# K^T transposes of an attention backward kernel issued one tick later on SyncE

## The chip, the cores and the metric

The kernel runs on one core of a Trainium2 chip. Its time is the device time of one execution in microseconds (us); the time before is the median of three runs, 1651.42 us (1650.91 to 1652.69). A profile and a trace of one further execution are at hand.

## The reference

Two independent attention blocks, A and B, are computed forward and differentiated. Each has x (8 x 96 x 640), key and value caches of 8 batches x 32 heads x 512 keys x 128, and the weights wq (640 x 4096) and wo (4096 x 640), all in bfloat16. The forward part of a block is

```
q      = (x @ wq) split into 32 heads of 128
scores = einsum("bhqd,bhkd->bhqk", q, k_cache) * 128 ** -0.5
p      = softmax(scores)
o      = einsum("bhqk,bhkd->bhqd", p, v_cache)
out    = (o, heads joined) @ wo
```

The kernel returns the two outputs side by side (8 x 96 x 1280) and, for a given grad_out of that shape, the gradients of x, k_cache, v_cache, wq and wo of both blocks (the vector-Jacobian product of this function).

## The kernel before

**Work items and ticks.** The unit of work is one (block, head, batch) triple: 2 x 32 x 8 = 512 items, each with 96 queries and 512 keys. A small class (`Emitter`) collects pieces of work under (tick, slot) and writes them out sorted by tick, then slot, then order of entry. One item starts per tick, so a head takes eight ticks, and a tick lasts about 1651 / 512 = 3.2 us on average. The table `OFF` says how many ticks before or after its item's own tick each stage of an item is issued, and `SLOTS` orders the stages in a tick. The items overlap as a software pipeline: while one item's scores are computed, others are in their later stages.

**Stages of an item.** K and V of two neighbouring batches, a pair, are loaded together (`c_ld`, 256 KB each; K five ticks ahead of the pair's tick, V three). Two operands are needed with the other axis on the partitions: K^T for the scores, V^T for dP. They are made by a DMA transpose from SBUF to SBUF, again for a pair at once (`c_xt`, L272 to L278, line L275 in the profile). For some items TensorE makes K^T instead, from the loaded K, with a copy by VectorE (`c_s1`): for the first pair of every head of even number, for all of head 0 of each block and for head 1 of block A (`k_on_pe`, L556). So 214 of the 256 pairs have a DMA transpose of K, and all 256 have one of V.

Three ticks after its own tick an item gets its scores (`c_s2a`, L298: S_ps<-KT,QT_h on TensorE, then the row maximum on VectorE), the exponential on ScalarE (L310), the reciprocal (L320, VectorE) and the scaled P (L329, GpSimd). Four ticks after: dV = P^T dO (L389), copied out by ScalarE (L392). Five: O^T from V and the transposed P (L359). Six: dP from V^T and dO (L417), then dS (L421). Seven: dK = dS^T Q (L432, copied out L435) and the transpose of dS. Eight: dQ^T from K (L340). Stores of dV and dK go out for a pair at a time, one tick after the second item's stage (`c_st`, L398).

**Work per head and per group.** Each head also has its slices of wq and wo loaded (L190, L199), transposed on TensorE and multiplied with x and grad_out (L243); later dwo (L469) and, for two heads at once, dwq (L490). The output and dx are summed over groups of about five heads (L514). These pieces sit in slot 90 and above, at the end of their ticks, so that ticks differ in length.

**SyncE's queue.** All DMAs are issued by SyncE, in the written order: most of them are pinned to it (`pinned`), and so are the transposes. Within a tick the loads of K and V come first (slot 0), then the transposes (slot 1), then the stores of dV and dK (1.5), the stores of dwo and dwq (1.6) and the loads of wq and wo (1.7). Heads start at odd ticks and pairs at every second tick, so V loads, K loads and dK stores fall in even ticks, and V^T transposes and dV stores in odd ticks. Before an issue SyncE waits until the data is there and the buffer free. Buffers are counted in pairs: seven for K, five for V, four each for K^T and V^T, four each for dK and dV.

Each transpose reads a tile of 128 x (2 x 4 x 128) and writes one of 128 x 8 x 128; a K^T buffer becomes free when the score matmuls of the pair four DMA transposes earlier are done, a V^T buffer when the dP matmuls of the pair four earlier are.

The table and the lines that place the transposes:

```
OFF = dict(ldk=-5, ldv=-3, kt=-3, vt=0, s2=3, s3=3, s4=4, s5=5, s6=6, s7=7, s8=8)
...
if not k_on_pe(h, b):
    em.add(ct + OFF["kt"], SLOTS["LOAD"] + 1, c_xt(h, b, "KT", 4))
em.add(ct + OFF["vt"], SLOTS["LOAD"] + 1, c_xt(h, b, "VT", 4))
```

Here `ct` is the tick of the pair's first item.

Of the kernel before, what the change touches and what calls it, by code (L numbers as in the profile page):

```python
# [41 lines left out]
SL_GRP = 95  # L42
SL_SETUP = 96

OFF = dict(ldk=-5, ldv=-3, kt=-3, vt=0, s2=3, s3=3, s4=4, s5=5, s6=6, s7=7, s8=8)
HK = dict(pA=-10, pA2=-9, pB=-3, pC0=[-2, 0], pC1=[-1, 0], pD1=1, pD0=2, qA0=18, qA1=17, qB=[19, 20], qD=[(18, 0, 2), (19, 2, 4), (21, 4, 5)])
EV = dict(pB0="act", pB1="dve", pC00="act", pC01="act", pC10="act", pC11="dve", pD0="dve", pD1="dve", qA0="act", qA1="dve", qB0="act", qB1="dve", qD="dve", gU="act")
GSPREAD0 = 9
# [5 lines left out]
def build_block(tc, em, tick0, blk, x, kc, vc, wq, wo, g_all, out_all, dx, dk, dv, dwq, dwo, ident, ones, pools, HG=6, first=True, groups=None):  # L54
# [207 lines left out]
    def c_ld(h, b, n, bufs):  # L262
        def f():
            src = kc if n == "K" else vc
            X = kvp.tile([128, NB, KC, 128], BF16, name=n + "_sb", bufs=bufs)
            pinned(nc.sync.dma_start(X[:], src[b:b + NB, h].rearrange("b (p c) d -> p b c d", c=KC)))
            for i in range(NB):
                st = CS.setdefault((blk, h, b + i), {})
                st[n + "_sb"], st[n + "_all"] = X[:, i], X
        return f  # L270

    def c_xt(h, b, name, bufs):  # L272
        def f():
            XT = kvp.tile([128, NB * KC, 128], BF16, name=name, bufs=bufs)
            pinned(nc.sync.dma_start_transpose(XT[:], CS[(blk, h, b)][name[0] + "_all"][:].rearrange("p a c d -> p (a c d)")))  # L275
            for i in range(NB):
                CS[(blk, h, b + i)][name] = XT[:, i * KC:(i + 1) * KC].rearrange("p c k -> p (c k)")
        return f  # L278

    def c_s1(h, b):  # L280
        def f():
            st = CS[(blk, h, b)]
            kT_ps = bank([128, Sk], BF16, "kT_ps")
            for c in range(KC):
                nc.tensor.transpose(kT_ps[:, c * 128:(c + 1) * 128], st["K_sb"][:, c, :], ident[:])
            KT = wk.tile([128, Sk], BF16, name="KT_pe", bufs=2)
            nc.vector.tensor_copy(KT[:], kT_ps[:])
            st["KT"] = KT[:]
        return f

    def c_s2a(h, b):
        def f():
            with tc.high_priority(PRIO_OFF):
                st = CS[(blk, h, b)]
                hs = HS[(blk, h)]
                tok = slice(b * Sq, (b + 1) * Sq)
                S_ps = bank([Sq, Sk], F32, "S_ps")
                nc.tensor.matmul(S_ps[:], hs["QT_h"][:, tok], st["KT"], start=True, stop=True)  # L298
                negm = wk.tile([Sq, 1], F32, name="negm", bufs=3)
                nc.vector.tensor_reduce(negm[:], S_ps[:], axis=AX.X, op=ALU.max, negate=True)  # L300
                st["S_ps"], st["negm"] = S_ps, negm
        return f

    def c_s2b(h, b):
        def f():
            with tc.high_priority(PRIO_OFF):
                st = CS[(blk, h, b)]
                E_sb = wk.tile([Sq, Sk], BF16, name="E_sb", bufs=2)
                rowsum = wk.tile([Sq, 1], F32, name="rowsum", bufs=3)
                nc.scalar.activation(E_sb[:], st["S_ps"][:], ACT.Exp, bias=st["negm"][:], scale=1.0, accum_out=rowsum[:])  # L310
                st["E_sb"], st["rowsum"] = E_sb, rowsum
                del st["S_ps"]
        return f

    def c_s3a(h, b):
        def f():
            with tc.high_priority(PRIO_OFF):
                st = CS[(blk, h, b)]
                rinv = wk.tile([Sq, 1], F32, name="rinv", bufs=3)
                nc.vector.reciprocal(rinv[:], st["rowsum"][:])  # L320
                st["rinv"] = rinv
        return f
# [233 lines left out]
    def k_on_pe(h, b):  # L556
        return (b // NB == 0 and h % 2 == 0) or h == 0 or (first and h == 1)

    SX = pools["SX"]
    for g in range(NG):  # L560
        h0 = GH0[g]
        for hh in range(groups[g]):
# [17 lines left out]
            for b in range(B):  # L580
                ct = c0t + b
                if b % NB == 0:
                    em.add(tick0 - 12 if first and h == 0 and b == 0 else ct + OFF["ldk"], SLOTS["LOAD"], c_ld(h, b, "K", 7))
                    em.add(ct + OFF["ldv"], SLOTS["LOAD"], c_ld(h, b, "V", 5))
# [3 lines that stand above are left out]
                if k_on_pe(h, b):  # L588
                    em.add(ct + 2, SLOTS["S1"], c_s1(h, b))
                em.add(ct + OFF["s2"], SLOTS["S2A"], c_s2a(h, b))  # L590
                em.add(ct + OFF["s2"], SLOTS["S2B"], c_s2b(h, b))
                em.add(ct + OFF["s3"], SLOTS["S3A"], c_s3a(h, b))
# [162 lines left out]
```

## Time and profile before

| what | value |
|---|---|
| time, median of 3 runs | 1651.42 us (1650.91 to 1652.69) |
| the profiled execution's own time | 1653.38 us |
| its span, first to last instruction | 1651.2 us |
| granted TensorE clock, mean | 0.998 |
| TensorE matmuls (PE) busy | 1633.2 us, 99% |
| ScalarE (ACT) / VectorE (DVE) / GpSimd (POOL) busy | 1391.9 / 1283.2 / 527.9 us |
| DMA: moved, mean rate | 447.11 MB, 271 GB/s |
| K^T transposes, issue to landing (median) | 4.7 us |
| V^T transposes, issue to landing (median) | 4.5 us |

The profile is of one execution. A line such as L275 is a line of the kernel; `out<-in` names the tile written and the tiles read. PE is TensorE's matmuls, PEld its weight loads; SPq is SyncE's queue, which only issues DMAs: the duration of such a row is the time that the issue took, and the data lands later. In lists in order of time the first column is the start in us from the span's start, the second the duration in us, and a bracket at the end tells how long the engine had been idle and what ended that. In lists of waits the numbers are the total in us, how often, and the longest. A busy TensorE isn't one at its peak, since the ends of matmuls are modelled.

### The profile page before, as it was taken

Reading aid. Unit: us, or ns where it says so; the run is one execution under the profiler, and the core shown is the slowest. Engines: PE = TensorE matmul, PEld = TensorE weight load, DVE = VectorE, ACT = ScalarE, POOL = GpSimd, SP = SyncE. Lnnn points to the kernel's source line nnn. Section 1 sums busy time; section 2 is a strip of 40 time slices with the busy share of each in tenths; the row PEclk is TensorE's granted clock in tenths of the full one; section 3 lists DMA queues with packets and bytes.
Section 4 is the critical chain, followed back from the end, with each engine's and each line's share of the span. In section 5 each row is a group of like instructions: output and inputs, shape, how many; then the busy total and the mean of one; then the engine's idle time right before and its main releaser. Section 6 shows DMA issues by size and latency. Waiting matters only on the chain.

```text
span 1651.2 us, 55679 instructions
## 1 busy us (share of the span) xinstructions
PE 1633.2 (99%) x21288; PEld 1303.0 (79%) x21288; DVE 1283.2 (78%) x2916; ACT 1391.9 (84%) x3518; POOL 527.9 (32%) x1034
## 2 busy tenths in 40 slices
PE   8999999999999999999999999999999999999999
PEld 6887787788788787887878877877877877877886
DVE  6886677788787787878878767778878778787777
ACT  6998898798798797988869998978977977987985
POOL 2332233232233232333323323323322322332332
PEclk9999999999999999999999999999999999999999
DMA  9999999999999999999999999999999999999995
GB/s 258 270 268 283 277 284 271 279 274 283 246 277 269 276 273 264 267 278 259 299 289 283 283 281 272 278 281 271 276 275 260 278 296 246 282 282 245 265 275 157
DMA packets 843947, 447.11 MB, mean 271 GB/s; under 512 B 516512, under 2 KB 843680, under 8 KB 843680
## 3 DMA queue, kind: packets, MB, share of 16 engines
q1 hardware_dynamic: 843680, 443.56, 110.8%
q8 instruction: 167, 2.74, 0.7%
q14 instruction: 100, 0.82, 0.1%
HBM read 161.09 MB, written 159.12 MB: 194 GB/s over the span
## 4 chain that ended last, share of the span: by engine, by line
PE 74%; ACT 15%; issue 5%; DVE 3%; DMA 2%; POOL 0%; SPq 0%; ACTq 0%; DVEq 0%; POOLq 0%
PE o_ps L514 12%; PE q_ps L243 10%; PE dwq_ps L490 6%; PE dK_ps L432 5%; PE dV_ps L389 5%; PE dP_ps L417 5%; PE S_ps L298 5%; PE dwo_ps L469 4%; PE dst_ps L346 4%; PE x_ps L365 4%; PE x_ps L359 4%; PE x_ps L340 4%; ACT dK_sb L435 3%; ACT E_sb L310 3%; ACT PT_sb L378 3%
## 5 line engine op out<-in xcount | busy, mean ns | idle before, releaser
L329 POOL TENSOR_SCALAR P_sb<-E_sb,rinv 96x512 bf16<-96x512 bf16 x512 | 353.6, 691 | 1096.3 <-DVE rinv L320 1062.1
L310 ACT ACTIVATE E_sb<-S_ps,negm 96x512 bf16<-96x512 f32 x512 | 354.4, 692 | 132.7 <-DVE negm L300 128.9
L421 DVE SCALAR_TENSOR_TENSOR dS_sb<-dP_ps,dl_ps,P_sb 96x512 bf16<-96x512 f32 x512 | 380.9, 744 | 46.7 <-PE dl_ps L419 42.4
L300 DVE TENSOR_REDUCE negm<-S_ps 96x1 f32<-96x512 f32 x512 | 347.5, 679 | 46.0 <-PE S_ps L298 43.9
L435 ACT ACTIVATE dK_sb<-dK_ps 128x512 bf16<-128x512 f32 x512 | 305.7, 597 | 89.1 <-PE dK_ps L432 88.1
L392 ACT ACTIVATE dV_sb<-dV_ps 128x512 bf16<-128x512 f32 x512 | 314.6, 614 | 0.0
L378 ACT ACTIVATE PT_sb<-x_ps 128x384 bf16<-128x384 bf16 x512 | 256.4, 501 | 0.0
L514 PEld LDWEIGHTS <-OD 128*128 128x128 bf16 x1536 | 135.7, 98 | 103.3 <-issue 1.3
L389 PE MATMUL dV_ps<-dOnat_h,P_sb 96*128 96x128 bf16 x2048 | 197.9, 219 | 1.0 <-DVE dOnat_h L160 0.6
L432 PE MATMUL dK_ps<-Qnat_h,dS_sb 96*128 96x128 bf16 x2048 | 197.8, 219 | 0.0
L417 PE MATMUL dP_ps<-VT,dOT_h 128*96 128x512 bf16 x512 | 195.3, 381 | 0.3
L407 POOL TENSOR_TENSOR prod<-OD,dOT_h 128x96 bf16<-128x96 bf16 x512 | 186.6, 364 | 9.2 <-ACT OD L375 8.2
L348 DVE COPY dST_sb<-dst_ps 128x384 bf16<-128x384 bf16 x512 | 177.1, 346 | 11.6 <-PE dst_ps L346 11.6
L320 DVE RECIPROCAL rinv<-rowsum 96x1 f32<-96x1 f32 x512 | 80.0, 156 | 133.3 <-ACT E_sb L310 128.6
L375 ACT ACTIVATE OD<-x_ps 128x192 bf16<-128x192 f32 (+1 forms) x515 | 171.4, 333 | 3.4 <-PE x_ps L340 3.4
L346 PE MATMUL dst_ps<-ident,dS_sb 96*128 96x96 bf16 x2048 | 171.8, 206 | 2.4 <-DVE dS_sb L421 0.2
L359 PE MATMUL x_ps<-PT_sb,V_sb 128*128 128x96 bf16 x2048 | 172.2, 206 | 0.5 <-ACT PT_sb L378 0.5
L365 PE MATMUL x_ps<-ident,P_sb 96*128 96x96 bf16 x2048 | 171.7, 205 | 0.5 <-POOL P_sb L329 0.3
L340 PE MATMUL x_ps<-dST_sb,K_sb 128*128 128x96 bf16 x2048 | 170.7, 206 | 0.0
L298 PE MATMUL S_ps<-KT,QT_h 128*96 128x512 bf16 x428 | 162.1, 379 | 1.1 <-DMA KT<-K_sb 0.7
L340 PEld LDWEIGHTS <-K_sb 128*128 128x128 bf16 x2048 | 133.3, 98 | 34.6
L514 PE MATMUL o_ps<-wo_h,OD 128*128 128x128 bf16 (+1 forms) x768 | 141.0, 299 | 0.0
(75 smaller groups left out, 3137.9 us busy)
## 6 DMA issues: line engine op xcount, KB each, us to landing
out_dram<-dV_sb SPq DMA_DIRECT2D x256, 256.0 KB, 3.5
out_dram<-dK_sb SPq DMA_DIRECT2D x256, 256.0 KB, 3.8
K_sb<-in_A_k_cache_dram SPq DMA_DIRECT2D x128, 256.0 KB, 4.1
V_sb<-in_A_v_cache_dram SPq DMA_DIRECT2D x128, 256.0 KB, 3.8
K_sb<-in_B_k_cache_dram SPq DMA_DIRECT2D x128, 256.0 KB, 4.1
V_sb<-in_B_v_cache_dram SPq DMA_DIRECT2D x128, 256.0 KB, 4.0
out_dram<-dwo_sb SPq DMA_DIRECT2D x64, 160.0 KB, 3.8
out_dram<-dwq_sb SPq DMA_DIRECT2D x32, 320.0 KB, 4.0
```

What stands on the lines that cost most here:

```text
L300: nc.vector.tensor_reduce(negm[:], S_ps[:], axis=AX.X, op=ALU.max, negate=True)
L310: nc.scalar.activation(E_sb[:], st["S_ps"][:], ACT.Exp, bias=st["negm"][:], scale=1.0, accum_out=rowsum[:])
L329: pinned(nc.gpsimd.tensor_scalar(P_sb[:], st["E_sb"][:], st["rinv"][:], 0.0, op0=ALU.mult, op1=ALU.add))
L340: nc.tensor.matmul(dQT_ps, st["K_sb"][:, c, :], st["dST_sb"][:, c * Sq:(c + 1) * Sq], start=(c == 0), stop=(c == KC - 1))
L378: nc.scalar.activation(PT_sb[:], PT_ps, ACT.Identity, scale=1.0)
L389: nc.tensor.matmul(dV_ps[:, c * 128:(c + 1) * 128], P_sb[:, c * 128:(c + 1) * 128], hs["dOnat_h"][:, b * 128:(b + 1) * 128], start=True, s ...
L392: nc.scalar.activation(SB[(blk, h, b // 2, "v")][:, b % 2], dV_ps[:], ACT.Identity, scale=1.0)
L417: nc.tensor.matmul(dP_ps[:], hs["dOT_h"][:, tok], st["VT"], start=True, stop=True)
L421: nc.vector.scalar_tensor_tensor(dS_sb[:], dP_ps[:], dl_ps[:, 0:1], st["P_sb"][:], op0=ALU.subtract, op1=ALU.mult)
L432: nc.tensor.matmul(dK_ps[:, c * 128:(c + 1) * 128], dS_sb[:, c * 128:(c + 1) * 128], hs["Qnat_h"][:, b * 128:(b + 1) * 128], start=True, s ...
L435: nc.scalar.activation(SB[(blk, h, b // 2, "k")][:, b % 2], dK_ps[:], ACT.Identity, scale=1.0)
L514: nc.tensor.matmul(o_ps[:], src[:, t * 128:(t + 1) * 128], rhs, start=(hh == 0), stop=(hh == groups[g] - 1))
```

## The change

K^T transposes are issued two ticks before their pair's tick instead of three. That is an odd tick, the one in which the V^T transpose of the pair before is issued, and in the same slot; the V^T transpose was entered first and comes first.

```diff
-OFF = dict(ldk=-5, ldv=-3, kt=-3, vt=0, s2=3, s3=3, s4=4, s5=5, s6=6, s7=7, s8=8)
+OFF = dict(ldk=-5, ldv=-3, kt=-2, vt=0, s2=3, s3=3, s4=4, s5=5, s6=6, s7=7, s8=8)
```

Nothing else differs. On SyncE the DMAs of two ticks, one pair of each kind, are then issued in this order (per-head loads and stores left out):

| before | after |
|---|---|
| V load | V load |
| K load | K load |
| **K^T transpose** | dK store |
| dK store | V^T transpose |
| V^T transpose | **K^T transpose** |
| dV store | dV store |

## The prediction

> **What bounds the kernel now.** I read the first part of the page (busy time by engine), then who waited for whom on TensorE, then the rows of the K^T tile, then the SyncE queue and TensorE in order of time at the tightest place.
>
> First part of the page: TensorE (PE) has work in 99% of the span, so 1651.2 - 1633.2 = 18.0 us is all that it idles, start and end included.
>
> ```profile
> PE 1633.2 (99%) x21288; PEld 1303.0 (79%) x21288; DVE 1283.2 (78%) x2916; ACT 1391.9 (84%) x3518; POOL 527.9 (32%) x1034
> ```
>
> Of the waits (us in all, times, longest), only these two are of TensorE for a K^T transpose: 2.0 us in three places. A change of the transposes can therefore win 2.0 us of waiting at most, and lose more.
>
> ```profile
> PEld L298 <- DMA KT<-K_sb: 1.3, 2, 1.0
> ...
> PE S_ps L298 <- DMA KT<-K_sb: 0.7, 1, 0.7
> ```
>
> The transposes by line, and the K^T tile: min, median and max of an issue in ns; the last line is us from issue to landing of K^T.
>
> ```profile
> L275 SPq DMA_TRANSPOSE VT<-V_sb x256: 1231/1384/3427, 12.2 to 1611.0; - x128
> L275 SPq DMA_TRANSPOSE KT<-K_sb x214: 1231/1236/2621, 47.9 to 1605.8; - x107
> ```
>
> ```profile
> DMA to landing us min/median/max: 3.2/4.7/6.9
> ```
>
> SyncE is nearly full too: its 1732 DMA issues take 1403 us of the 1651, and the 16 DMA engines are busy over 90% in all but the last slice. So SyncE runs late in stretches where TensorE's ticks are short. SyncE in order of time (start, duration) at the worst of them:
>
> ```profile
> 938.85 0.42 SPq L266 DMA_DIRECT2D K_sb<-in_B_k_cache_dram  x1
> 939.32 1.34 SPq L275 DMA_TRANSPOSE KT<-K_sb  x1
> 940.76 0.56 SPq L398 DMA_DIRECT2D out_dram<-dK_sb  x1
> 941.37 0.65 SPq L199 DMA_DIRECT2D wo_h<-in_B_wo_dram  x1
> 942.12 3.04 SPq L275 DMA_TRANSPOSE VT<-V_sb  x1
> 945.25 0.53 SPq L398 DMA_DIRECT2D out_dram<-dV_sb  x1
> ```
>
> and TensorE at its end:
>
> ```profile
> 944.80 0.30 PE L469 MATMUL dwo_ps<-g_nat,Onat 128*128 128x320 bf16 x1
> 945.85 0.42 PE L298 MATMUL S_ps<-KT,QT_h 128*96 128x512 bf16 x1 [0.75 <-DMA KT<-K_sb]
> ```
>
> The K^T issued at 939.32 lands at 945.80 (6.48 us, a piece of the chain that ended last), and its score matmul starts at 945.85. Six ticks were planned between them; here 6.5 us, some two ticks, are left, and TensorE waits already.
>
> I paired every K^T landing with the first score matmul that reads it (both are in program order in the trace) and call the time between them the margin: median 8.6 us, under 4 us for 23 of 214, smallest 0.04. The small ones come in stretches: score matmuls at 106 to 143 us (smallest margin 0.64, at 122.6), 508 (2.71), 906 to 960 (0.12 at 926.5, 0.04 at 938.3 and 945.8), 1072 to 1085 (2.86), 1578 (2.83).
>
> **The change, part by part.** It removes and adds nothing; TensorE, ScalarE, VectorE and GpSimd keep their orders. Moved are 214 DMA transposes on SyncE's queue, each one tick later. Built, the order of a pair goes from V load, K load, K^T, dK store, V^T, dV store to V load, K load, dK store, V^T, K^T, dV store.
>
> 1. What K^T is moved past: the dK store (median issue 0.57 us, gap 0.09) and V^T (1.38, gap 0.09), 2.1 us, and once in a head each a wo load or a dwo store (0.5 to 0.7). Row by row (from the dK store's start to V^T's end, with its waits, and 0.09) the issue moves by 2.0 to 3.9 us, median 2.6. At 939.32: 945.15 + 0.09 - 940.76 = 4.5.
>
> 2. What is moved forward: dK stores and V^T, by the K^T issue of 1.2 us. V^T's smallest margin to the dP matmul is 2.9 us and grows; dK buffers are rewritten 1.2 us or more after their store landed. Both are already covered, so this wins nothing: V^T's cover is its six ticks to the dP matmul. The dV store, the next V and K loads keep their place: the same issues stand ahead of them.
>
> 3. Waits. V^T waits for the dP matmul that frees its buffer; K^T now stands behind that wait. In the trace V^T's issue met a real wait of this kind five times (3.5 us in all): 45 of 256 K loads are held by TensorE instead (57 us), and V^T follows 2.4 us behind. After the change V^T follows only 1.1 us behind and will be held more often, but only where SyncE has caught up, and there the K^T margin is above 6 us. It is no cost while margins stand so; if not, it is up to 1.3 us on the K^T behind it.
>
> 4. What it costs. The loss of a stretch is the largest (delay - margin) in it, not the sum: once TensorE is late by that much, the later transposes of the stretch have that much more. Two rows price the delay, neither of them a K^T behind a V^T, which the trace does not show.
> By the issue, each K^T keeping its own time from issue to landing: 2.97 - 0.64 = 2.33 at 122.6; 3.32 - 2.71 = 0.61 at 508.2; 4.48 - 0.04 = 4.44 at 945.8; 3.88 - 2.83 = 1.05 at 1578.4; others negative or covered. Sum 8.4 us.
> By the landing: K^T's issue now ends when V^T's did, with the same work issued ahead, so it lands when V^T did: 1.75 (at 129.3), 1.99 (at 945.8: V^T landed at 947.84) and 0.69 (at 1071.6). Sum 4.4 us.
> The place in the queue speaks for the second, K^T's longer time from the end of issue to landing (median 3.16 us against 2.74) for the first. I take the middle, 6.4 us. Ends: V^T's issue at its shortest, 1.23 us, because no K^T is just ahead of it, with K^T's own landing: 4.9; less than 4.4 if the landings come closer together, down to nothing. Upward: K^T landing as its slowest tenth does, 4.5 us after the issue (+1.35): 16.9; and if SyncE is held back by the late TensorE, so that each of the 13 places pays for itself by the first pricing: 20.9.
>
> The Trainium skill, "Advanced Engine Details and Errata", section on the X-Bar transpose (TRN2), says that transpose DMAs are as fast as regular ones. The trace's packets differ: 1,024 of 256 B at 18 ns for a transpose, 256 of 1,024 B at 46 ns for a copy of the same 256 KB, on 16 engines 1.15 us against 0.74. By that rule V^T would put 0.41 us less in front of K^T in each of the four stretches of the first pricing, and that sum would be 8.4 - 1.6 = 6.8 us.
>
> Against the profiled execution (1653.38 us, span 1651.2 and 2.2 around it) the sum is 1659.8. That execution lies 2.0 us above the median of the three runs, 1651.42, so on the median: 1651.4 + 6.4 = 1657.8. Under 0.2% (3.3 us), a change can't be told from none.
>
> **Rivals.**
> - Hidden anyway, not slower: the transposes in the crowded stretches are held by the DMA engines, not by the queue. At 939.32 the K^T's first packets run only from 942.3, and nearly all engines then stand still from 942.8 to 944.7 in its middle. If that standstill falls on V^T when V^T goes first, K^T lands right behind it and only the 0.12 and 0.04 margins pay. For: it is a single piece of 2 us in the worst place. Against: V^T in front then passes the standstill on to K^T, which waits in the same queue. It decides if K^T lands less than about 1.5 us later at 926.5 to 945.8; time: 0 to 3 us more, 1653.
> - Larger: two transposes in a row, each 1,024 small packets, land later than one behind copies. For: V^T issued within 0.8 us of a K^T has 2.5 us or more of issue in one case of ten, against 1.4 where 4 us or more lie between. Against: its median there is 1.38. With 2 us on every K^T landing the stretches cost 22 us, with 4 us 41 us: 1673 to 1693.
> - Faster: V^T's issue is above its shortest by 91 us in all, K^T's by 40. If the new order sheds much of it, SyncE is less late and all margins grow. For: 4 copies now stand between a K^T and the next V^T. Against: K^T takes V^T's place right behind a transpose, and TensorE has 2.0 us of such waits to give back: 1649.4 at best, within 0.2%. More than that would need gains on ScalarE or VectorE that no row shows.
>
> **How the numbers follow.** Forecast, 3.3 to 17 us slower: 0.58. Larger, over 17 us: 0.14. Hidden, within 0.2%: 0.22. Faster by over 0.2%: 0.06. So slower 0.72, same 0.22, faster 0.06. The range leaves out the faster case with the lower half of the standstill case, and the upper part of the larger one: 1651.5 to 1674.
>
> **What would show it.** Right: TensorE's waits at L298 for K^T grow from 2.0 us to 5 to 10, in the stretches 106 to 143, 906 to 960 and perhaps 508, 1072 and 1578, not spread evenly; K^T lands 2 to 3 us later against its score matmul (median margin near 6); K^T's issue takes over V^T's excess. Wrong: no L298 waits (hidden), L298 waits in every head (larger), or other lines of TensorE waiting for V, K or wo loads.

## The result, and the profile after

The changed kernel takes 1720.35 us, the median of 4 runs (1714.02 to 1731.27), against 1652.06 us, the median of four runs of the kernel before: a ratio of 1.0413, 95% interval 1.0384 to 1.0441. It is 68 us slower where 6.4 were forecast, and outside the range. The profiled execution took 1716.21 us, its span is 1714.0 us, 62.8 more than before.

First part of the page of the changed kernel, busy time by engine:

```profile
PE 1639.6 (96%) x21107; PEld 1309.6 (76%) x21288; DVE 1288.9 (75%) x2916; ACT 1396.6 (81%) x3518; POOL 528.5 (31%) x1034
```

TensorE now idles for 74.4 us of the span and not 18.0. (181 matmul records are missing from this trace. A kernel shown below, two_between, has the same gaps in its records and takes as long as before, and its PE reads 1622.4 us, some 11 too low. So of the 74.4 us some 11 aren't idle.) Its work is some 17 us longer than that kernel's; the granted clock, 0.992 against 1.000 there, makes 13 of these. And the lower clock follows from the waits: between the first and the last 10 us it drops to half seven times, six times for 3.4 us and once for 6.8, and each drop directly follows a stretch of 3.4 us in which TensorE idled for 2.05 us or more in a wait for K^T. (From 130.0 to 133.4 us it works for 1.35 us; from 133.4 to 136.8 the granted clock is 0.50.) Of the stretches of 3.4 us with no drop behind them none has more than 1.88 us of idle time. The kernel before has no drop between 11 and 1649 us.

The waits of the changed kernel say what TensorE idles for (us in all, times, longest):

```profile
PEld L298 <- DMA KT<-K_sb: 51.1, 29, 4.5
...
PE S_ps L298 <- DMA KT<-K_sb: 42.2, 25, 4.3
```

So the line was forecast rightly, K^T ahead of the score matmul at L298: on the weight load, which waits first, 1.3 us became 51.1. (The matmul's 42.2 us are the later part of the same waits.) The chain that ended last, its shares by engine before and after, has more DMA now and less ScalarE:

```profile
PE 74%; ACT 15%; issue 5%; DVE 3%; DMA 2%; POOL 0%; SPq 0%; ACTq 0%; DVEq 0%; POOLq 0%
```

```profile
PE 74%; DMA 11%; ACT 8%; DVE 3%; issue 3%; SPq 0%; POOL 0%; ACTq 0%; DVEq 0%; POOLq 0%
```

The transposes by line, and the last line of the K^T tile's view, from issue to landing:

```profile
L275 SPq DMA_TRANSPOSE KT<-K_sb x214: 1299/1977/4129, 48.5 to 1676.8; - x107
```

```profile
L275 SPq DMA_TRANSPOSE VT<-V_sb x256: 1237/1494/3182, 11.7 to 1679.9; - x128
```

```profile
DMA to landing us min/median/max: 3.2/4.7/6.2
```

Here are two surprises. A K^T takes no longer from issue to landing, 4.7 us as before. But its issue, now right behind a V^T, takes 1.98 us in the median and not 1.24, while V^T's median did not get shorter (1.49 us after, 1.38 before). A pair on SyncE in order of time, at an ordinary place of the changed kernel:

```profile
712.95 0.42 SPq L266 DMA_DIRECT2D V_sb<-in_A_v_cache_dram  x1
713.46 0.45 SPq L266 DMA_DIRECT2D K_sb<-in_A_k_cache_dram  x1
714.00 0.95 SPq L398 DMA_DIRECT2D out_dram<-dK_sb  x1
715.04 1.30 SPq L275 DMA_TRANSPOSE VT<-V_sb  x1
716.40 1.89 SPq L275 DMA_TRANSPOSE KT<-K_sb  x1
718.39 0.53 SPq L398 DMA_DIRECT2D out_dram<-dV_sb  x1
```

Each row starts 0.06 to 0.10 us after the end of the one before it, so SyncE waits for nothing but its own issues here; the next pair's V load starts at 719.01, 6.06 us after this one. I added up all rows of SyncE; a wait is what a gap ahead of an issue has above the usual 0.09 us. Before: 1403.4 us of issues and 97 us of waits for other engines, 53 of them ahead of K loads, for TensorE to free the buffer. After: 1525.6 us of issues (K^T 303 to 457, V^T 406 to 388, all others -14) and 38 us of waits, 7 of them ahead of K loads. Issues +122, waits -59: +63 us, which is the span's 62.8. That the sum comes out proves nothing, since SyncE issues from the first us to the last; it says where its time went, and whether the longer issues are the cause is for the experiments to show. The rest of the account is in what follows: why the same 1732 DMAs keep the queue longer.

The margin (landing of a K^T to its first score matmul) has a median of 3.2 us, against 8.6 before, and is under 4 us for 126 of 214, against 23. The move by itself explains 2.6 us of that.

### The profile page after: what moved, and what is told of

It is laid out like the page before. It is cut to its first block, busy times and chain, and to the rows that moved or that the text cites. A ratio compares the mean times of both kernels' runs of the same rounds, so it can differ in the third digit from the quotient of the medians.

```text
span 1714.0 us, 55491 instructions
## 1 busy us (share of the span) xinstructions
PE 1639.6 (96%) x21107; PEld 1309.6 (76%) x21288; DVE 1288.9 (75%) x2916; ACT 1396.6 (81%) x3518; POOL 528.5 (31%) x1034
## 4 chain that ended last, share of the span: by engine, by line
PE 74%; DMA 11%; ACT 8%; DVE 3%; issue 3%; SPq 0%; POOL 0%; ACTq 0%; DVEq 0%; POOLq 0%
PE o_ps L514 11%; PE q_ps L243 10%; DMA KT<-K_sb 8%; PE dwq_ps L490 5%; PE S_ps L298 5%; PE dwo_ps L469 5%; PE dK_ps L432 5%; PE dV_ps L389 5%; PE dP_ps L417 5%; PE dst_ps L346 4%; PE x_ps L340 4%; PE x_ps L365 4%; PE x_ps L359 4%; PE n_ps L258 2%; ACT E_sb L310 2%
## 5 line engine op out<-in xcount | busy, mean ns | idle before, releaser
L298 PE MATMUL S_ps<-KT,QT_h 128*96 128x512 bf16 x428 | 164.2, 384 | 44.0 <-DMA KT<-K_sb 42.2
L469 PE MATMUL dwo_ps<-g_nat,Onat 128*128 128x320 bf16 x768 | 137.4, 304 | 1.5 <-ACT E_sb L310 0.7
```

## The experiments: lateness or order

In all tables and lines below the kernels are named as in their headings. "Issues" and "waits" are SyncE's rows added up as above; of the margin two values are given, the one that a tenth of the 214 lies under, and the median.

**apart_late.** The changed kernel with K^T behind the dV store: V, K, dK, V^T, dV, K^T. K^T is still later, but no transpose has another right ahead of it.

```diff
-em.add(ct + OFF["kt"], SLOTS["LOAD"] + 1, c_xt(h, b, "KT", 4))
+em.add(ct + OFF["kt"], SLOTS["LOAD"] + 1.56, c_xt(h, b, "KT", 4))
```

> The changed kernel with K^T one place later still, behind the dV store, so that one store stands between V^T and K^T. Two theories. Neighbours: the loss comes from a transpose that is issued right behind another (its issue takes 1.98 us instead of 1.24, SyncE's queue fills up). Then this is near the kernel before, 1652 to 1662 us, K^T's issue median falls below 1.4 us, and waits at L298 are below 15 us. Late: the loss comes from K^T being one tick later. Then this is at least as slow as the changed kernel, 1715 us or more, with waits at L298 of 40 us or more.

**neighbours_early.** The kernel before with the dK store a tick later (and the small DMAs of a head moved out of the way, two further lines that are left out here): V, K, K^T, V^T, dK, dV. The transposes are neighbours, but K^T stands where it stood.

```diff
-em.add(ct + OFF["s7"] + 1, SLOTS["LOAD"] + 1.5, c_st(h, b, "k"))
+em.add(ct + OFF["s7"] + 2, SLOTS["LOAD"] + 1.2, c_st(h, b, "k"))
```

> The kernel before with K^T in its old place, and V^T moved to stand right behind it (the dK store, and the wo load and dwo store of that tick, moved out from between). K^T is no later than before. Neighbours: 1695 to 1730 us, V^T's issue median near 2.0 us, waits of TensorE for K^T all the same, because SyncE's whole queue is late. Late: 1650 to 1655 us.

**two_between.** The kernel before with the dV store ahead of V^T: V, K, K^T, dK, dV, V^T.

```diff
-em.add(ct + OFF["s4"] + 1, SLOTS["LOAD"] + 1.5, c_st(h, b, "v"))
+em.add(ct + OFF["s4"] + 1, SLOTS["LOAD"] + 0.5, c_st(h, b, "v"))
```

> The kernel before with the dV store ahead of V^T, so that two stores stand between K^T and V^T, and two loads between V^T and the next K^T. K^T is where it was. Neighbours: V^T's issue median falls from 1.38 to about 1.25 us, SyncE gets some slack, 1647 to 1652 us; the smallest margins grow. Late: nothing changes, 1651 to 1653 us.

**swapped.** The changed kernel with K^T ahead of V^T: V, K, dK, K^T, V^T, dV. K^T is issued a V^T earlier than after the change.

```diff
-em.add(ct + OFF["kt"], SLOTS["LOAD"] + 1, c_xt(h, b, "KT", 4))
+em.add(ct + OFF["kt"], SLOTS["LOAD"] + 0.9, c_xt(h, b, "KT", 4))
```

> The changed kernel with K^T ahead of V^T in the tick that they share: neighbours as before, K^T earlier by one transpose (1.5 us) than in the changed kernel. Neighbours: 1700 to 1725 us, V^T's issue near 2.0 us now and K^T's near 1.3. Late: about half the loss is gone, 1670 to 1690 us.

Measured:

| kernel | ratio (95%) | span | issues | waits (K loads) | margin |
|---|---|---|---|---|---|
| before | 1 | 1651.2 | 1403 | 97 (53) | 3.65, 8.64 |
| after | 1.0413 (1.0384 to 1.0441) | 1714.0 | 1526 | 38 (7) | 0.04, 3.21 |
| apart_late | 1.0325 (1.0286 to 1.0364) | 1697.9 | 1501 | 46 (11) | 0.04, 3.83 |
| neighbours_early | 1.0200 (1.0175 to 1.0225) | 1686.2 | 1495 | 40 (3) | 0.64, 4.86 |
| two_between | 1.0002 (0.9993 to 1.0011) | 1650.9 | 1432 | 68 (20) | 3.45, 7.91 |
| swapped | 1.0468 (1.0443 to 1.0494) | 1729.8 | 1538 | 40 (7) | 0.04, 3.21 |

apart_late (1704.58 us) and neighbours_early (1686.66) lie between the ranges of the two theories, swapped (1731.02) above both; two_between (1652.42) is in the range of lateness.

Waits for K^T of swapped, where K^T is issued ahead of V^T, and of neighbours_early, where it has its old place in the order:

```profile
PEld L298 <- DMA KT<-K_sb: 59.2, 39, 3.2
```

```profile
PEld L298 <- DMA KT<-K_sb: 20.3, 16, 3.1
```

Lateness fell as the cause: with K^T in its old place the kernel still loses 35 us, and K^T moved forward from the new place wins nothing back (1722.61 to 1734.15 us in four runs, against 1714.02 to 1731.27). "Neighbours" as the only cause fell too, by apart_late. In neighbours_early the V^T is the one behind a transpose, and its issue is now the longer one, 1.77 us in the median:

```profile
L275 SPq DMA_TRANSPOSE VT<-V_sb x256: 1231/1774/4230, 12.1 to 1648.5; - x128
L275 SPq DMA_TRANSPOSE KT<-K_sb x214: 1231/1238/2988, 48.4 to 1643.5; - x107
```

What goes with the time in all six rows is the sum of the issues: an order makes the whole queue slower or not, and each slow order has used up the waits ahead of the K loads. Once these are gone the span can only follow the sum, so the table doesn't yet say which of the two drives the other.

## The experiments: is the queue the bound

If so, work taken off the queue must give the time back without touching K^T's place, and work added to the kernel before must cost the same with the order untouched.

**half_dk.** The changed kernel without the dK store of every second pair, 128 of 256; half of the K gradients aren't written.

```diff
-em.add(ct + OFF["s7"] + 1, SLOTS["LOAD"] + 1.5, c_st(h, b, "k"))
+if b % 4 == 3:
+    em.add(ct + OFF["s7"] + 1, SLOTS["LOAD"] + 1.5, c_st(h, b, "k"))
```

> The changed kernel without the dK store of every second pair (that half of the gradients of k_cache is left unwritten): 0.65 us of the queue and 0.74 us of the DMA engines less per two pairs, order otherwise as changed. Speed: the queue has its slack back, 1650 to 1668 us, K loads wait for TensorE again (30 us or more). Position: K^T is as late as before the edit in half of the pairs, 1690 to 1715 us.

**extra_store.** The kernel before, with the dV of every second pair stored a second time, to a scratch tensor.

```diff
+if which == "v" and b % 4 == 3:
+    pinned(nc.sync.dma_start(pools["scratch"][blk, h, b // 4].rearrange("b (p c) d -> p b (c d)", c=KC), t[:]))
```

> The kernel before with the dV store of every second pair done a second time, to a scratch tensor in DRAM: order and K^T's place as in the kernel before, 0.63 us of the queue and 0.74 us of the DMA engines more per two pairs (some 80 to 95 us over the run, against 97 us that SyncE waits for semaphores now). Speed: that slack is used up and the kernel loses time, 1665 to 1710 us, with waits of TensorE for K^T at L298. Position: K^T is where it was, 1650 to 1658 us.

**pair_earlier.** The changed order, but K loads and K^T a whole pair earlier, with one K buffer more (and, for its room, four staging buffers in place of five).

```diff
-OFF = dict(ldk=-5, ldv=-3, kt=-2, vt=0, ...)
+OFF = dict(ldk=-7, ldv=-3, kt=-4, vt=0, ...)
```

> The changed kernel's order with K loads and K^T transposes a pair of ticks earlier (K loads seven ticks ahead, K^T four; eight K buffers instead of seven, four stage buffers instead of five): V^T and K^T are neighbours as in the changed kernel, but K^T has two more ticks than there and one more than in the kernel before. Position: the loss is gone, 1650 to 1660 us. Speed: the queue passes a pair no faster, so the lag grows until K^T is late all the same, 1680 to 1715 us.

| kernel | ratio (95%) | span | issues | waits (K loads) | margin |
|---|---|---|---|---|---|
| half_dk | 1.0036 (1.0025 to 1.0047) | 1657.5 | 1421 | 97 (44) | 1.62, 6.19 |
| extra_store | 1.0400 (1.0376 to 1.0424) | 1718.6 | 1527 | 34 (6) | 0.04, 3.29 |
| pair_earlier | 1.0469 (1.0442 to 1.0496) | 1728.4 | 1537 | 37 (5) | 1.03, 5.25 |

half_dk keeps the changed order, with K^T behind V^T and its long issue, and the waits are gone but for these:

```profile
PEld L298 <- DMA KT<-K_sb: 6.3, 4, 3.5
```

```profile
L275 SPq DMA_TRANSPOSE KT<-K_sb x214: 1260/1759/4361, 50.7 to 1612.6; - x107
```

extra_store keeps the order and the K^T's short issue of the kernel before, and has the waits of the changed kernel:

```profile
PEld L298 <- DMA KT<-K_sb: 56.8, 36, 4.4
```

```profile
L275 SPq DMA_TRANSPOSE KT<-K_sb x214: 1237/1250/2680, 46.0 to 1678.7; - x107
```

pair_earlier gives K^T its margin back, and the waits go to whatever else the queue brings late (ScalarE for dK buffers whose store hasn't landed, TensorE for the wo loads):

```profile
ACT dK_sb L435 <- DMA out_dram<-dK_sb: 47.6, 33, 3.8
PEld L210 <- DMA wo_h<-in_B_wo_dram: 25.4, 11, 3.3
PE woT_ps L210 <- DMA wo_h<-in_B_wo_dram: 22.1, 10, 3.0
```

half_dk (1659.83 us) is in its range for a slow queue; extra_store (1720.66) and pair_earlier (1731.25) lost more than theirs allow, and far more than the ranges for K^T's place.

So after the change SyncE's queue, with the DMA engines behind it, is the bound, and which line shows the wait is only a matter of what is needed first. The runs do not separate SyncE's issuing from the engines' transfers. The account holds roughly: taking 128 stores away gave 56.5 us of span and 37 us of new K-load waits, 0.73 us a store; adding 128 cost 67.4 us and 47 of the old waits, 0.89.

## The experiments: what makes an order slow

Kernels that only move: loads, transposes and stores of the pairs in ten phases of 25 pairs, each phase in one of the orders, with nothing else on SyncE. The gradients aren't computed in them. The time of a phase, per pair, is read from the starts of its issues, the first four pairs left out.

```
ORDERS = {
    "before": "V K kt dk vt dv",
    "after": "V K dk vt kt dv",
    ...
for _ in range(83):
    nc.tensor.matmul(warm_ps[:], warm[:, 0:128], warm[:], start=True, stop=True)
```

The last two lines, matmuls that depend on no DMA, are in alone_matmuls and the runs after it only; dma_alone has none, and alone_act_dve has ScalarE, VectorE and GpSimd work in their place.

For dma_alone:

> The DMAs of a pair alone, no other work: SyncE issues K and V loads, both transposes and two stores (of constant tiles) in the orders of the kernels so far, 25 pairs of each order one after the other; the per-head loads and stores are left out, and the gradients are not computed. Read from the trace: us per pair by order, for orders before, after, apart and late, neighbours early, two between, swapped, without transposes. Theory speed: the order sets how fast the queue and the DMA engines pass a pair; before takes about 5.9 us, after and swapped 0.2 to 0.5 us more, two between as before. Theory position: all orders take the same within 1%, and only K^T's place counts.

For alone_matmuls:

> The DMAs alone again (orders one after the other, 25 pairs each, no gradients computed), now beside an idle stream of 83 matmuls a pair on TensorE that touch nothing of theirs: it brings the instruction fetches of the kernel (one of 16 KB for some 128 matmuls with their weight loads), which the run of the DMAs alone had none of. Theory fetches: a fetch holds one DMA engine and a transpose waits for all engines, and this costs more where two transposes and four copies stand in a row; then the orders part here as they do in the kernel: before 6.0 to 6.2 us a pair, changed, swapped and neighbours early 0.2 to 0.5 us more. Theory elsewhere (memory ports, semaphore waits, per-head DMAs): all orders stay within 2% of one another, 5.6 to 5.9 us.

For alone_act_dve:

> The DMAs alone, beside free-running ScalarE, VectorE and GpSimd work of the kernel's shapes (8, 7 and 3 operations a pair, no matmuls, no gradients computed), so without the instruction fetches of TensorE. Theory fetches: as alone, 5.6 to 5.9 us a pair in all orders. Theory ports: slower by 0.3 us or more, and more so where transposes are neighbours.

For double_fetch:

> The DMAs alone beside 166 small matmuls a pair instead of 83 (no gradients computed; orders before and changed in turn, five times 25 pairs each): twice the instructions of TensorE, so about twice the instruction fetches a pair, while TensorE runs. Theory fetches: the price doubles, before from +0.2 to about +0.4 us a pair over the DMAs alone (6.2 to 6.3), changed from +0.5 to about +1.0 (6.7 to 6.9). Theory that the matmuls slow the DMAs in another way, by their reads: the operands are smaller here, so both orders stay at or below the 6.0 and 6.35 us of the run with 83.

For half_fetch:

> The DMAs alone beside matmuls again, ten phases of 25 pairs, the outputs not computed; but 42 matmuls of 320 columns a pair in place of 83 of 160: the same work of TensorE in half the instructions, so half the 16 KB instruction packets (some 82 for 162). If the instruction packets make the orders part: half the price, the order before 5.9 us a pair, after 6.05 to 6.15, a difference of 0.1 to 0.25. If TensorE's own work (its reads and writes) does: as with 83 matmuls, 6.0 and 6.35, a difference of 0.25 to 0.4.

Microseconds per pair, each number the mean of the phases in that order (two phases of one order differ by up to 0.24, in double_fetch by 0.29):

| order | dma_alone | alone_act_dve | half_fetch | alone_matmuls | double_fetch |
|---|---|---|---|---|---|
| 16 KB packets in all | 0 | 0 | 82 | 162 | 324 |
| before | 5.83 | 5.81 | 5.85 | 6.01 | 6.41 |
| after | 5.80 | 5.92 | 5.89 | 6.35 | 7.02 |
| swapped | 5.82 | 5.78 | 5.90 | 6.26 | |
| neighbours_early | 5.56 | 5.50 | 5.77 | 6.13 | |
| apart_late | 5.91 | 6.07 | 5.70 | 6.41 | |
| two_between | 5.76 | 5.68 | 5.99 | 6.04 | |

(TensorE ended in the last phases, which are left out: 6.13 for swapped in alone_matmuls, 6.15 for after in double_fetch.) Without transposes a pair takes 2.76.

My first idea, that the orders differ by themselves, fell with dma_alone: before and after take the same. Work of the other three engines beside them does not part them either: 5.81 and 5.92 in alone_act_dve, and 5.79 and 5.99 in the first phase of each, where all three still worked (GpSimd's work ended at 536 us, ScalarE's at 984, VectorE's at 1196), so within the scatter. With matmuls beside them they part, by 0.34 us a pair: 5.98 and 6.05 for before, 6.40 and 6.30 for after. What matmuls bring to the DMA engines is their instructions. The queues of dma_alone, alone_matmuls, half_fetch and double_fetch in that order (packets, MB, share of 16 engines):

```profile
q14 instruction: 12, 0.10, 0.0%
```

```profile
q8 instruction: 162, 2.65, 0.7%
```

```profile
q8 instruction: 82, 1.34, 0.4%
```

```profile
q8 instruction: 324, 5.31, 1.3%
```

These are packets of 16 KB, 1.08 us each on one engine. half_fetch does the same work on TensorE (1428.9 us busy, 1437.9 in alone_matmuls) in half the instructions, and the difference between before and after falls from 0.34 to 0.04; double_fetch has twice the instructions with smaller matmuls, and it is 0.61. So it goes with the number of instructions, and with their packets, and not with TensorE's work. It is not in proportion: for half the packets 0.1 to 0.25 was expected, and 0.04 is within the scatter. Both kernels have the same number of them, one each 10 us (page of the kernel before):

```profile
q8 instruction: 167, 2.74, 0.7%
```

In the traces of before and after a transpose in whose time such a packet falls has its packets spread over 2.3 to 2.7 us, against 1.1 to 1.6, in both kernels alike, and the core's rate drops from 290 to 150 GB/s for 1 to 2 us. In the kernel before it then rises to some 325 and catches up; in the kernel after it stays below 290.

Which property of an order decides that, more orders should have told, each beside 83 matmuls.

> The DMAs alone beside 83 matmuls a pair (no gradients computed) in further orders, to see which property of an order makes the fetches dear. Theory spacing: the even order with two copies between transposes (both ways) is cheapest, 5.9 to 6.0, transposes in a row dearest, 6.3 or more. Theory what-stands-ahead: a transpose right behind a load is cheap and one right behind a store or a transpose dear: dv kt / K vt mixed; V kt K vt and V kt, K vt (both behind loads) 5.7 to 6.0; dk kt, dv vt (both behind stores) 6.3 or more, whether one or three copies or two and two stand between.

| order | us per pair |
|---|---|
| V K kt dk vt dv (before) | 6.10, 5.92 |
| V kt K vt dk dv | 5.91, 5.42 (TensorE ended early in the second) |
| dk V kt dv K vt | 6.02, 6.02 |
| V dk kt K dv vt | 6.04 |
| dk dv kt V K vt | 6.35 |
| V K dk dv kt vt | 6.66 |
| dk kt dv vt V K | 8.18 (K^T waits for the K just loaded: 24 waits, 70 us) |

No single property sorts them: two transposes behind two stores are dearest, but "two copies between" stands at 6.02 and at 6.35, and a K^T behind a store at 6.04. That stays open.

## The experiments: how near the edge

**kt_first.** The kernel before in the cheapest order of the last table: V, K^T, K, V^T, dK, dV.

```diff
-OFF = dict(..., kt=-3, vt=0, ...)
+OFF = dict(..., kt=-3, vt=1, ...)
...
-em.add(ct + OFF["kt"], SLOTS["LOAD"] + 1, c_xt(h, b, "KT", 4))
-em.add(ct + OFF["vt"], SLOTS["LOAD"] + 1, c_xt(h, b, "VT", 4))
+em.add(ct + OFF["kt"], SLOTS["LOAD"] + 0.2, c_xt(h, b, "KT", 4))
+em.add(ct + OFF["vt"], SLOTS["LOAD"] + 0.4, c_xt(h, b, "VT", 4))
```

(The K load stands at 0.3.)

> The kernel before with another order on SyncE: V load, K^T transposes, K load, V^T transposes, dK store, dV store. K^T stands two places earlier and its tick is the same; V^T follows a load and not a store. With TensorE's instruction stream beside them, the DMAs alone took 5.91 us a pair in this order against 6.10 in the order before. If the time of the queue is what the orders differ in, also inside the kernel: 1648 to 1653 us, since TensorE's own 1643 us are then the bound, and SyncE's idle waits, 97 us before, grow to 120 or more, nearly all of them for buffers of the loads. If what the DMAs alone show does not carry over to the kernel (a transposition with another right behind it is dear in every case): SyncE's waits under 60 us and 1665 us or more.

**before_fewer_pe**, the kernel before, and **kt_first_fewer_pe**, the one above: 30 of the 42 pairs whose K^T TensorE transposes itself go to the DMA. (The expectations below have 36 pairs and 480 matmuls; the counts of the traces give 256 - 214 = 42 pairs, and 240 matmuls with as many weight loads.)

```diff
-return (b // NB == 0 and h % 2 == 0) or h == 0 or (first and h == 1)
+return h == 0 or (first and h == 1)
```

For before_fewer_pe:

> The kernel before in its own order, with the same 30 pairs moved from TensorE to the DMA transposition. The queue had 53 us of waits for the K loads' buffers before; 30 more transposes cost it 40 to 60 us. If the kernel before lies at the edge of what SyncE's queue carries: 1655 to 1690 us, with TensorE waiting for K^T in 20 us or more. If there is slack left in it: 1638 to 1646 us, TensorE's saving alone.

For kt_first_fewer_pe:

> The order of the run before it, and of the 36 pairs whose K^T TensorE transposes itself, 30 are moved to the DMA transposition: 480 fewer matmuls and 30 more pairs of K^T transposes on SyncE. If the order leaves the queue slack (by the DMAs alone some 0.2 us a pair, 50 us in all) and TensorE is the bound: TensorE's work falls by 480 instructions at 20 to 30 ns, 10 to 14 us, and the time is 1637 to 1645 us. If the queue is at its edge with this order too: 30 more transposes at 1.5 us or more of the queue, 45 us, of which the slack covers a part: 1655 to 1680 us.

| kernel | ratio (95%) | span | issues | waits (K loads) |
|---|---|---|---|---|
| kt_first | 1.0023 (1.0013 to 1.0033) | 1655.1 | 1404 | 105 (36) |
| before_fewer_pe | 1.0003 (0.9982 to 1.0023) | 1644.2 | 1446 | 45 (7) |
| kt_first_fewer_pe | 1.0093 (1.0079 to 1.0106) | 1664.8 | 1456 | 61 (5) |

kt_first, at 1656.13 us between its two ranges, saved the queue nothing against the order before (1404 us of issues and 1403), so the small differences among the alone runs don't carry over. before_fewer_pe is the edge itself: 30 more transposes used up the K loads' waits, 53 to 7 us. All waits fell by 52 us and the span by 7, so they cost the queue 45 us, what 30 transposes cost in dma_alone (5.83 - 2.76 for two, 1.53 us each, 46 us). TensorE has 12 us less to do,

```profile
PE 1621.2 (99%) x21048; PEld 1288.2 (78%) x21048; DVE 1265.9 (77%) x2856; ACT 1388.1 (84%) x3518; POOL 526.6 (32%) x1034
```

and the profiled execution has a span 7 us shorter; but its ten runs lie between 1645.45 and 1665.90 us where eighteen of the kernel before lie between 1651.26 and 1656.36. My range for the edge, 1655 and more, was too high. In kt_first_fewer_pe the queue is the bound and V^T, which this order brings last, is what TensorE waits for:

```profile
PEld L417 <- DMA VT<-V_sb: 17.1, 13, 2.2
```

None of the versions beats the kernel before by more than can be measured.

## Why the prediction was wrong

- **What bounds the kernel now.** TensorE, right: half_dk and two_between end at its work. But the prediction read the full SyncE (1403 of 1651 us) only as "late in stretches". The number to set beside it was the idle time of the queue, 97 us, 53 of them at K loads, and what the new order does to the sum of the issues: 59 us of that idle time was used up, and 63 more came on top.
- **Step 1, what K^T is moved past.** 2.6 us in the median, taken from the trace before. Of the margin's loss of 5.4 us it can be 2.6; the rest is SyncE behind with everything.
- **Step 2, "The dV store, the next V and K loads keep their place": this is the step that failed.** They keep their place in the order, not in time. It took the sum of SyncE's issues as given and moved terms about in it. K^T's issues grew by 154 us and V^T's shrank by 18: the excess was not taken over, it was added.
- **Step 3, waits.** V^T "will be held more often, but only where SyncE has caught up": SyncE hardly catches up any more. The waits ahead of the K loads fell from 53 to 7 us, and no pause in the queue restores the margins.
- **Step 4, what it costs.** Delay less margin was summed over four stretches, 8.4 and 4.4 us, on the margins of before. A queue that is late nearly throughout doesn't keep to four stretches: the 30 waits of over 0.1 us lie between 111 and 1648 us, in 12 of the 18 stretches of 100 us. The upper end, 20.9, let each of 13 places pay for itself, and no end of the range priced a longer queue. The step that should have been there: issues +122, less the waits used up, 59: +63.
- **Rivals.** Hidden and faster were excluded. The standstill that the hidden case rested on, 942.8 to 944.7, is not the single piece it was taken for: an instruction packet of 16 KB starts at 942.31, with the first packets of that K^T, and some 140 of the 470 transposes of that trace have such a packet in their time. Larger, "two transposes in a row land later", had the sign and came nearest, with 1673 to 1693, but not the mechanism: K^T lands 4.7 us after its issue as before, and swapped, with K^T first of the two, is no faster. It said "in every head", which isn't so either: 30 waits in 64 heads.
- **The Trainium skill**, "Advanced Engine Details and Errata", section on the X-Bar transpose (TRN2): transpose DMAs as fast as regular ones. In dma_alone a 256 KB transpose costs 1.53 us and a copy 2.76 / 4 = 0.69. The measurement decides; here the rule is off by a factor of 2.2, and the sum that the prediction made by it, 6.8, missed as far as the others.
- **What would show it.** L298 waits and a K^T issue of its neighbour's length were named, with 5 to 10 us for the waits; 51.1 came on the weight load alone. (The 2.0 us of before are two places and not three: the matmul's 0.7 us are part of the weight load's wait at 945.85, so 1.3 us is what TensorE lost.) A median margin "near 6" was 3.2.

Shown: that the queue's time, not K^T's place, makes the loss (neighbours_early, swapped, half_dk, extra_store, pair_earlier), and that, with the DMAs alone, the orders before and after part with the number of TensorE's instructions and their packets (dma_alone, half_fetch, alone_matmuls, double_fetch). That the packets do it in the kernel too is argued, from the rates behind a packet in the traces of before and after. By alone_matmuls the change costs 0.34 us a pair, 87 us in 256 pairs; in the kernel it is 63 us of span and 46 of the K loads' waits, 109. For swapped and neighbours_early the same account gives 125 and 85 us, by the alone runs 64 and 31, but for apart_late 89 and 102: in the kernel these two orders with neighbours are dearer than alone, and why isn't settled. Nor is it why an order with K^T right behind V^T doesn't catch up after an instruction packet.

## What to carry to other kernels

Before moving a DMA in a queue that is near full, add up the queue's issues and its waits for others, and ask what the new order does to the sum: the waits are all that hides a slower queue, and once they are used up, the margins shrink everywhere and not only where they were tight (median 8.6 to 3.2 us here). Where a transfer is late, look whether the queue is ever idle; if it isn't, an earlier place only hands the wait to the next transfer, and only fewer transfers or a cheaper order help. In this kernel the three orders in which two transposes stand next to each other all lost time, but one without neighbours did too (apart_late). So measure an order in the running kernel, since DMAs by themselves don't show its price.

## What the runs showed of the hardware

- TensorE's instruction stream travels through the same 16 DMA engines: 167 packets of 16 KB, 0.7% of their time, and a transpose in flight beside one spreads its packets over 2.3 to 2.7 us in the median, against 1.1 to 1.6 without. (Part of that may be that a longer transpose is likelier to meet one.) The stream is told by its count: half and twice the matmuls have 82 and 324 such packets, against 162.
- The price of an order on one queue depends on that stream: before and after differ by -0.03, 0.04, 0.34 and 0.61 us a pair with 0, 82, 162 and 324 such packets, where two phases of one order differ by up to 0.29.
- The issue of a transpose right behind another takes 1.76 to 1.98 us in the median (half_dk, neighbours_early, swapped, after), behind a store 1.36 to 1.56 (before_fewer_pe, before, swapped, apart_late), behind a load 1.24 to 1.44 (before, kt_first).
- The busy share of the DMA engines says little of what is left: it is over 90% in all slices of before, after and dma_alone but the last of the first two, at 271, 261 and 276 GB/s.
- The granted clock of TensorE drops to half for 3.4 us right after a stretch of 3.4 us with 2.05 us or more of idle time, in the trace of the changed kernel seven times; one stretch with 1.88 us had no drop behind it. In swapped and extra_store twenty more drops follow 1.78 us or more, and one stretch with 2.00 us has none, so where the limit lies isn't settled.
